# The first quarter of block 0's feed-forward done by groups of 128 tokens, the first group moved ahead of two weight scales

## Chip, cores, metric

One core of one Trainium2 chip. The metric is the device time of one execution in microseconds, the median of several runs; a profile is one more execution of the same program.

## What is computed

Causal softmax attention over 4 batches, 8 heads, 576 tokens, head width 64, mixed per head with a linear-memory read-out, and then a two-matrix feed-forward with squared ReLU over all 2304 tokens:

```
a = softmax(causal(q @ k.T / sqrt(D)));  local = a @ v
mem = (phi(q) @ M_prev) / (phi(q) @ z_prev + 1e-6)
x = (g * mem + (1 - g) * local)            # [2304, 512]
out = square(relu(x @ w_in)) @ w_out       # w_in [512, 2048], w_out [2048, 512]
```

Inputs are float32; the output must hold float32 accuracy, so the big products are made of float16 pairs (a high and a low half of each operand, three products each).

## The kernel before

**Weights.** `w_in` and `w_out` arrive as 32 pieces of 512 KB (lines 180 to 185): pieces 0 to 3 are the first quarter of the columns of `w_in`, 4 to 7 the rows of `w_out` that belong to it, 8 to 15 the second quarter, and so on. Each piece is loaded from SP's queue (`load_weight`, L273), turned to float32 on ACT and DVE (`to_float`, L198 to L203), and, four pieces at a time, PE forms a bound of the magnitudes (`gr`, L229, then L210) from which DVE makes a scale (L232 to L241). Only then `halves` (L247 on ACT, L248 on DVE) writes the float16 pair `w`. From piece 16 on the pieces use smaller rings of buffers, opened after piece 15.

**Attention.** 16 units, each a batch and a pair of heads (the first eight are cut in two by query tiles). A unit forms scores (`sp`, L586), masks them with a running maximum (L607 on DVE), exponentiates (L627 on ACT), and for the first units transposes the result on PE (`pxa`, L642), copies it (`aF`, L647 on ACT), multiplies by v (`acc`, L691) and adds into `feat` (L694). `pm` (L550) is the memory read-out. PSUM has one buffer for `sp` and two each for `up`, `acc`/`oacc` and `av`.

**Feed-forward.** `moe(n)` does a block of 256 tokens. Block 0 is the first 64 tokens of every batch, which `first_tokens` computes on its own in two groups of 128; each group's result `hl` is transposed by a DMA (L413) into its half of `xT`. Per pair of 128 hidden columns (`j`), PE does 24 products of 128x128 by 128x256 into `up` (L976 to L978), ACT does ReLU, square and a rounding to float16 (`r`, `gh`: L982, L983, L985), DVE the low half (`gl`, L988), and `down` does 12 products with 512 columns into `oacc` (L947 to L949). In block 0 every quarter (two `j`) is scaled and summed on its own (`group_sum`, L953).

**Order.** A scheduler places the instructions on each engine at build time, from the order in which the generators emit them; `ORD` (L88) merges them by ratios: attention unit 0 with half of the weight steps, then units 1 to 3 with the rest and the steps of block 0 (`first`), then the other units; blocks 1 to 8 come after. At run time each engine takes its list in order and waits where an input is late.

Of the kernel before, what the change touches and what calls it, by code (L numbers as in the profile page):

```python
# [8 lines left out]
F32 = mybir.dt.float32  # L9
F32R = mybir.dt.float32r  # L10
F16 = mybir.dt.float16
# [11 lines left out]
P = 128  # L23
# [36 lines left out]
RB = 2  # L60
# [18 lines left out]

FIRST = 4  # L80
WA = 0
WE = 8
WE2 = 40
AFTER = mybir.DependencyInfo(mybir.DependencyClass.NoSync, mybir.DependencyReason.DATA)
# [1 line left out]


def ORD(merge, attn, na, wsteps, first, order):  # L88
    merge((attn(0, 1), 12), (wsteps(17), 16))
    merge((attn(1, FIRST), 52), (wsteps(34), 16), (first(), 18))  # L90
    for _ in attn(FIRST, len(order)):
        pass

# [6 lines left out]
def fused_kernel(ctx: ExitStack, tc: tile.TileContext, t0_d, kk_d, qv_d, beta, w_in, w_out, out):  # L100
# [85 lines left out]
    def w_out_op(f, part):  # L186
        return wt[8 * (f // 4) + 4 + f % 4][:, part, :]
# [737 lines left out]
    def moe(n):  # L925
        b, blk = blocks[n]
        xT, osc = xq[n]
        x0 = xT.rearrange("p g (x b m) (h q) -> p g x b m h q", x=2, b=GB, h=2)
        pend = []

        def x_op(k, part):

            return x0[:, :, part, :, k // 2, k % 2] if lead else xT[:, :, part * NK + k]

        acc = []
        lead = b is None
        outs = []

        def down(j, gh, gl):
            if j == 0 or lead and j % 2 == 0:  # L940
                acc[:] = [ps.tile([P, DM], F32, tag="acc", name="oacc", bufs=2) for t in range(2)]
            f0, f1 = (j // 2 * 4, j // 2 * 4 + 3) if lead else (0, NF - 1)
            last = j == NF // 2 - 1 or lead and j % 2
            for u, t in [(u, t) for t in range(2) for u in range(2)] if last else [(u, t) for u in range(2) for t in range(2)]:
                f = 2 * j + u
                ts = slice(t * P, (t + 1) * P)
                nc.tensor.matmul(acc[t], gh[:, u, ts], w_out_op(f, 0), start=f == f0, stop=False)  # L947
                nc.tensor.matmul(acc[t], gh[:, u, ts], w_out_op(f, 1), start=False, stop=False)  # L948
                nc.tensor.matmul(acc[t], gl[:, u, ts], w_out_op(f, 0), start=False, stop=f == f1)  # L949
            if lead and j % 2:  # L950
                group_sum(j // 2)

        def group_sum(jj):  # L953
            kj = mo.tile([P, 2], F32, tag="kj", name="kj", bufs=2)
            kp = kap[:, jj : jj + 1]
            nc.vector.tensor_scalar(
                out=kj, in0=tok0, scalar1=kp, scalar2=kp, op0=ALU.mult, op1=ALU.mult
            )
            for t in range(2):
                if jj == 0:  # L960
                    o = mo.tile([P, DM], F32, tag="x", name="o", bufs=XB)
                    outs.append(o)
                    nc.scalar.activation(o, acc[t], AF.Copy, scale=kj[:, t : t + 1])
                else:
                    nc.vector.scalar_tensor_tensor(
                        out=outs[t], in0=acc[t], scalar=kj[:, t : t + 1], in1=outs[t], op0=ALU.mult, op1=ALU.add
                    )

        for j in range(NF // 2):
            need(1 + 8 * (j // 2 + 1))  # L970
            up = ps.tile([P, 2, BLK], F32, tag="up", name="up", bufs=2)
            for u in range(2):
                f = 2 * j + u
                uo = up[:, u].rearrange("p (g b q) -> p g b q", g=2, b=GB) if lead else up[:, u]
                for k in range(NK):
                    nc.tensor.matmul(uo, w_in_op(f, k, 0), x_op(k, 0), start=k == 0, stop=False)  # L976
                    nc.tensor.matmul(uo, w_in_op(f, k, 0), x_op(k, 1), start=False, stop=False)  # L977
                    nc.tensor.matmul(uo, w_in_op(f, k, 1), x_op(k, 0), start=False, stop=k == NK - 1)  # L978
            r = mo.tile([P, 2, BLK], F32, tag="r", name="r", bufs=RB)
            gh = mo.tile([P, 2, BLK], F16, tag="gh", name="gh", bufs=GHB)  # L980
            gl = mo.tile([P, 2, BLK], F16, tag="gl", name="gl", bufs=GLB)
            nc.scalar.activation(r, up, AF.Relu, scale=HSC if lead else gam[:, j // 2 : j // 2 + 1])  # L982
            nc.scalar.activation(r, r, AF.Square)  # L983
            if n < GHN:
                nc.scalar.copy(gh, r)  # L985
            else:
                nc.vector.tensor_copy(gh, r)
            (nc.vector if n in GLV else nc.gpsimd).tensor_tensor(out=gl, in0=r, in1=gh, op=ALU.subtract)  # L988
            pend.append((j, gh, gl))
            yield  # L990
            if len(pend) > 1:
                down(*pend.pop(0))
                yield
        for x in pend:
            down(*x)
            yield
        for t in range(2):
            if lead:
                for u in range(2):
                    r0 = (2 * t + u) * S  # L1000
                    nc.sync.dma_start(out[r0 : r0 + D, :], outs[t][u * D : (u + 1) * D])
            else:
                o = mo.tile([P, DM], F32, tag="x", name="o", bufs=XB)
                nc.scalar.activation(o, acc[t], AF.Copy, scale=osc[:, t : t + 1])
                r0 = b * S + QT[1 + 2 * blk + t][0]
                nc.sync.dma_start(out[r0 : r0 + P, :], o)
        yield
# [5 lines left out]
    def merge(*parts):  # L1013
        live = [[g, n, 0] for g, n in parts]
        while live:
            live.sort(key=lambda x: (x[2] + 0.5) / x[1])
            if next(live[0][0], "end") == "end":
                live.pop(0)
            else:
                live[0][2] += 1  # L1020
# [6 lines left out]
    def need(n):  # L1027
        while wn[0] < n:
            next(wg)
            wn[0] += 1  # L1030

    def wsteps(n):
        for k in range(n):
            if wn[0] < n:
                need(wn[0] + 1)
            yield
# [22 lines left out]
    def attn(i0, i1):  # L1059

        ahead = []
        for i in range(i0, i1):
            rows = ahead.pop() if ahead else unit(i)
            if i >= WA:
                for x in (rows,) if i == i0 else ():
                    for _ in iter(lambda: next(x), "whole"):
                        yield
                if i + 1 < i1:
                    ahead.append(unit(i + 1))
                    for _ in iter(lambda: next(ahead[0]), "whole"):  # L1070
                        yield
            yield from rows
            b, p, tiles = order[i]
            if p == NP - 1:
                need(NU + 2)
                for blk in range(2):
                    if 2 * blk + 1 in tiles and b < B - 1:
                        prefetch(b, blk)
                yield
# [65 lines left out]
```

## Time and profile before

| | |
|---|---|
| median of 3 runs | 566.0 us (564.21 to 567.09) |
| the profiled execution, own time | 562.5 us |
| its span | 560.7 us |
| PE busy | 519.1 us (93%) |
| DVE busy | 453.0 us (81%) |
| ACT busy | 410.7 us (73%) |

Busy time is a union of instructions, and a matmul's shown duration is longer than the step to the next one, since they are pipelined. A step is read from the starts of two neighbours. PEclk is the share of full speed that PE's clock was granted: 1.00 or 0.50, and a value between in a window that holds both.

### The profile page before, as it was taken

To read this page: it belongs to the slowest core of one execution; us is meant where nothing else is said; L and a number is where in the kernel's file an instruction comes from. 1 tells how busy PE (TensorE), PEld (TensorE's weight loads), DVE (VectorE), ACT (ScalarE), POOL (GpSimd) and SP (SyncE) were. 2 spreads that over 40 slices of the span, in tenths; PEclk is the share of its full clock that TensorE was granted. 3 is DMA by queue.
4 is the path that set the end of the run, shared out by engine and by line. 5 is a ranking of instruction groups with operands and counts; after the bars stand their busy time and mean duration, and the time that the engine had idled before them with its cause. 6 is when DMAs were issued, how large, how long until landed. Compare 5 with 4: busy or idle time off the path is not lost.

```text
span 560.7 us, 12604 instructions
## 1 busy us (share of the span) xinstructions
PE 519.1 (93%) x4767; PEld 367.1 (65%) x4767; DVE 453.0 (81%) x1421; ACT 410.7 (73%) x884; POOL 16.6 (3%) x20
## 2 busy tenths in 40 slices
PE   4658987999998999999989989999999999999997
PEld 3546755657676766667767757766766766447766
DVE  6898689998988889898968878887786788745645
ACT  3799899796888879799777778887576734566252
POOL 1001000011010000000000000000000000000000
PEclk9767999999999999999999999999999999999999
DMA  8952972488567657978558466482645330100002
GB/s 311 404 162 60 368 280 61 91 172 206 116 155 160 167 136 140 187 162 202 119 103 160 108 134 123 76 136 61 109 84 77 86 57 1 39 1 1 1 1 75
DMA packets 133132, 71.37 MB, mean 127 GB/s; under 512 B 115408, under 2 KB 121552, under 8 KB 133072
## 3 DMA queue, kind: packets, MB, share of 16 engines
q1 hardware_dynamic: 133072, 70.57, 52.2%
q8 instruction: 37, 0.61, 0.4%
q14 instruction: 23, 0.19, 0.1%
HBM read 37.53 MB, written 4.72 MB: 75 GB/s over the span
## 4 chain that ended last, share of the span: by engine, by line
PE 36%; DVE 29%; ACT 19%; DMA 11%; issue 3%; SPq 0%; POOL 0%; ACTq 0%; DVEq 0%
DVE e L607 5%; DVE a L667 5%; ACT e L627 5%; DMA aT<-a 4%; PE seven L844 4%; PE oacc L949 3%; PE up L976 3%; PE oacc L948 3%; PE oacc L947 3%; PE up L978 3%; PE up L977 3%; ACT a L665 3%; PE seven L815 2%; PE seven L817 2%; PE seven L816 2%
## 5 line engine op out<-in xcount | busy, mean ns | idle before, releaser
L976 PE MATMUL up<-xT,w 128*128 128x256 f16 x448 | 122.6, 274 | 0.7 <-DMA xT<-hl 0.7
L977 PE MATMUL up<-xT,w 128*128 128x256 f16 x448 | 122.6, 274 | 0.0
L978 PE MATMUL up<-xT,w 128*128 128x256 f16 x448 | 122.5, 273 | 0.0
L627 ACT ACTIVATE e<-e,mx 128x320 f32<-128x320 f32 (+3 forms) x128 | 77.4, 606 | 44.4 <-DVE feat L694 25.1
L947 PE MATMUL oacc<-w,gh 128*128 128x512 f16 x224 | 84.8, 379 | 3.4 <-ACT gh L985 3.3
L948 PE MATMUL oacc<-w,gh 128*128 128x512 f16 x224 | 84.9, 379 | 0.0
L949 PE MATMUL oacc<-w,gl 128*128 128x512 f16 x224 | 81.7, 379 | 1.4 <-DVE gl L988 1.4
L667 DVE SCALAR_TENSOR_TENSOR a<-e,a 128x128 f16<-128x128 f32 x116 | 64.6, 566 | 12.3 <-ACT a L665 11.7
L665 ACT ACTIVATE a<-e 128x128 f16<-128x128 f32 x116 | 54.9, 522 | 3.6 <-DMA aT<-a 3.3
L976 PEld LDWEIGHTS <-w 128*128 128x128 f16 x448 | 43.9, 98 | 11.1 <-DMA xT<-hl 0.8
L977 PEld LDWEIGHTS <-w 128*128 128x128 f16 x448 | 44.0, 98 | 10.6 <-issue 0.8
L691 PE MATMUL acc<-vs,aT 128*128 128x64 f16 x1138 | 42.9, 193 | 6.6 <-DMA aT<-a 5.9
L978 PEld LDWEIGHTS <-w 128*128 128x128 f16 x448 | 44.0, 98 | 6.5 <-issue 0.4
L607 DVE CUSTOM_DVE_ANT_0 e<-sp,mask 128x320 f32<-128x320 f32 (+3 forms) x128 | 47.0, 417 | 0.8 <-PE pxa L642 0.4
L691 PEld LDWEIGHTS <-aT 128*128 128x128 f16 x1138 | 38.7, 98 | 13.2 <-DMA aT<-a 8.3
L982 ACT ACTIVATE r<-up,gam 128x512 f32<-128x512 f32 x48 | 32.3, 674 | 20.2 <-PE up L978 20.1
L988 DVE TENSOR_TENSOR gl<-r,gh 128x512 f16<-128x512 f32 x56 | 38.7, 691 | 4.3 <-ACT gh L985 3.6
L949 PEld LDWEIGHTS <-gl 128*128 128x128 f16 x224 | 21.7, 98 | 24.9 <-DVE gl L988 2.6
L947 PEld LDWEIGHTS <-gh 128*128 128x128 f16 x224 | 21.9, 98 | 23.6 <-ACT gh L985 4.5
L844 PEld LDWEIGHTS <-g 128*128 128x128 f16 x336 | 32.7, 98 | 5.4 <-DVE g L770 1.2
L983 ACT ACTIVATE r<-r 128x512 f32<-128x512 f32 x56 | 34.9, 624 | 0.8
L948 PEld LDWEIGHTS <-gh 128*128 128x128 f16 x224 | 21.9, 98 | 19.8
(192 smaller groups left out, 1035.4 us busy)
## 6 DMA issues: line engine op xcount, KB each, us to landing
raw<-in_w_in_dram SPq DMA_DIRECT2D x16, 512.0 KB, 7.1
raw<-in_w_out_dram SPq DMA_DIRECT2D x16, 512.0 KB, 7.9
vv<-in_qv_dram SPq DMA_DIRECT2D x16, 320.0 KB, 3.2
kd<-in_kk_dram SPq DMA_DIRECT2D x16, 288.0 KB, 3.1
out_dram<-o SPq DMA_DIRECT2D x12, 256.0 KB, 2.2
qm<-in_qv_dram SPq DMA_DIRECT2D x8, 321.0 KB, 3.2
qm<-in_qv_dram SPq DMA_DIRECT2D x8, 193.0 KB, 2.9
vv<-in_qv_dram SPq DMA_DIRECT2D x8, 192.0 KB, 3.1
```

Of the source, the lines that this page charges most:

```text
L607: nc.vector.tensor_tensor_reduce(out=e[:, h, ka:kb], in0=sps[:, h, cs], in1=mask[:, 448 - q0 + ka : 448 - q0 + kb], scale=-0.125, scalar=3 ...
L627: ex = nc.scalar.activation(e[:n, h, :ke], e[:n, h, :ke], AF.Exp, bias=bs, scale=-1.0, accum_out=sm[:n, h : h + 1])
L665: nc.scalar.mul(av[:, :, o0 : o0 + w], x, SC)
L667: nc.vector.scalar_tensor_tensor(out=av[:, :, o0 + w : o0 + 2 * w], in0=x, scalar=SC, in1=av[:, :, o0 : o0 + w], op0=ALU.mult, op1=ALU.sub ...
L691: nc.tensor.matmul(acc[:n, h], lhs[:, :n], rhs, start=x == 0, stop=x == len(mms) - 1)
L844: mms.append(nc.tensor.matmul(x[:, blk], g[j][:, i0, a, blk, p], t_side(j, p, m, i1), start=j == js[0] and p == n == 0, stop=j == js[-1] a ...
L947: nc.tensor.matmul(acc[t], gh[:, u, ts], w_out_op(f, 0), start=f == f0, stop=False)
L948: nc.tensor.matmul(acc[t], gh[:, u, ts], w_out_op(f, 1), start=False, stop=False)
L949: nc.tensor.matmul(acc[t], gl[:, u, ts], w_out_op(f, 0), start=False, stop=f == f1)
L976: nc.tensor.matmul(uo, w_in_op(f, k, 0), x_op(k, 0), start=k == 0, stop=False)
L977: nc.tensor.matmul(uo, w_in_op(f, k, 0), x_op(k, 1), start=False, stop=False)
L978: nc.tensor.matmul(uo, w_in_op(f, k, 1), x_op(k, 0), start=False, stop=k == NK - 1)
```

## The change

Block 0's first quarter (`NQG = 1`) is done by `by_groups`: for each group of 128 tokens, 48 products with 128 moving columns into one `up` bank, the three ACT passes and the DVE pass over 128x512, then 12 products with 512 columns into an accumulator of the group's own, and its sum. Before, the same quarter was two `j` of 24 products with 256 columns. `group_sum` now takes one group at a time. `ORD` lets the first step of block 0 (the first group's `up` products and passes) come after unit 0 and 9 weight steps, that is ahead of the steps of pieces 9 to 15 in the emitted order; units 1 and 2 to 3 are merged in two separate parts.

```
+NQG = 1
 def ORD(merge, attn, na, wsteps, first, order):
-    merge((attn(0, 1), 12), (wsteps(17), 16))
-    merge((attn(1, FIRST), 52), (wsteps(34), 16), (first(), 18))
+    f = first()
+    merge((attn(0, 1), 12), (wsteps(9), 8))
+    next(f)
+    merge((attn(1, 2), 17), (wsteps(17), 8))
+    merge((attn(2, FIRST), 35), (wsteps(34), 16), (f, 17))
...
+        def by_groups(jj):
+            def sum_up(g, gh, gl):
+                y = ps.tile([P, DM], F32, tag="acc", name="accg", bufs=2)
+                for u in range(4):
+                    f = 4 * jj + u
+                    nc.tensor.matmul(y, gh[:, u], w_out_op(f, 0), start=u == 0, stop=False)
+                    nc.tensor.matmul(y, gh[:, u], w_out_op(f, 1), start=False, stop=False)
+                    nc.tensor.matmul(y, gl[:, u], w_out_op(f, 0), start=False, stop=u == 3)
+                group_sum(jj, g, y)
+            for g in range(2):
+                up = ps.tile([P, 4, P], F32, tag="up", name="upg", bufs=2)
+                for u in range(4):
+                    f = 4 * jj + u
+                    uo = up[:, u].rearrange("p (b q) -> p b q", b=GB)
+                    for k in range(NK):
+                        hi, low = (x0[:, g, x, :, k // 2, k % 2] for x in range(2))
+                        nc.tensor.matmul(uo, w_in_op(f, k, 0), hi, start=k == 0, stop=False)
+                        nc.tensor.matmul(uo, w_in_op(f, k, 0), low, start=False, stop=False)
+                        nc.tensor.matmul(uo, w_in_op(f, k, 1), hi, start=False, stop=k == NK - 1)
+                r = mo.tile([P, 4, P], F32, tag="r", name="rg", bufs=RB)
...
+                nc.scalar.activation(r, up, AF.Relu, scale=HSC)
+                nc.scalar.activation(r, r, AF.Square)
+                nc.scalar.copy(gh, r)
+                nc.vector.tensor_tensor(out=gl, in0=r, in1=gh, op=ALU.subtract)
+                yield
+                sum_up(g, gh, gl)
+                yield
...
         for j in range(NF // 2):
             need(1 + 8 * (j // 2 + 1))
+            if lead and j // 2 < NQG:
+                if j % 2 == 0:
+                    yield from by_groups(j // 2)
+                continue
```

In the built order the lists are equal up to PE's first `pm`. Line numbers of the changed kernel are higher by 4 up to `moe`; its new names end in g. Three places follow.

On PE, after unit 0's read-out `pm`, the list before goes on with the bounds of pieces 8 to 13 (`gr`, 24 products):

```order
L586 MATMUL sp<-kd,qm 128x192 x2
L550 MATMUL pm<-qm,pe 128x130 x2
L229 LDWEIGHTS fc
L229 MATMUL gr<-fc 128x128
L229 LDWEIGHTS fc
```

and of the change, at the same place:

```order
L554 MATMUL pm<-qm,pe 128x130 x2
L994 LDWEIGHTS w_488
L994 MATMUL upg<-xT,w_488 128x128
L995 LDWEIGHTS w_488
L995 MATMUL upg<-xT,w_488 128x128
L996 LDWEIGHTS w_488
L996 MATMUL upg<-xT,w_488 128x128
```

There 29 of the first group's 48 products stand now; the other 19 follow between unit 1's scores and transposes, and the first `gr` of piece 8 comes after the 48th.

On ACT, between unit 0's four exponentials and the halves of the second quarter of `w_in`, before:

```order
L627 ACTIVATE e,sm<-e,mx 128x192 x2
L416 ACTIVATE tok_80<-qn 64x1 x2
L409 ACTIVATE hl<-f,sn 128x256 x2
L647 COPY aF<-pxa 64x128 x2
L647 COPY aF<-pxa 128x256 x2
L247 ACTIVATE w_609<-fc,win_s 128x512
```

and of the change:

```order
L631 ACTIVATE e,sm<-e,mx 128x320
L1000 ACTIVATE rg<-upg 128x512
L631 ACTIVATE e,sm<-e,mx 128x320
L1001 ACTIVATE rg<-rg 128x512
L651 COPY aF<-pxa 64x128 x2
L651 COPY aF<-pxa 128x128 x2
L1002 CAST ghg<-rg 128x512
L631 ACTIVATE e,sm<-e,mx 128x192 x2
L251 ACTIVATE w_744<-fc,win_s 128x512
```

The first group's three passes, unit 1's first exponentials and unit 0's second set of copies stand ahead of the halves now.

Also on ACT, between the second quarter's halves of `w_in` and those of `w_out`, where before one followed directly on the other:

```order
L251 ACTIVATE w_753<-fc,win_s 128x512
L495 ACTIVATE pe<-qm 128x256
L968 ACTIVATE o<-accg,kj 128x512
L651 COPY aF<-pxa 64x128 x2
L651 COPY aF<-pxa 128x256
L251 ACTIVATE w_797<-fc,wout_s 128x512
```

A copy out of the first group's accumulator and copies of unit 1 came between them.

## Rows read from the trace of the kernel before

**Rows 1.** The page's parts 1 and 2: busy time, and PE in 40 slices.
```profile
PE 519.1 (93%) x4767; PEld 367.1 (65%) x4767; DVE 453.0 (81%) x1421; ACT 410.7 (73%) x884; POOL 16.6 (3%) x20
PE   4658987999998999999989989999999999999997
```
**Rows 2.** Busy time by stretch; columns: stretch, length, PE, PEld, DVE, ACT, POOL, PEclk, DMA, GB/s.
```profile
28.00:42.00 14.00, 7.32 (x70) 5.62 (x72) 13.26 (x34) 13.96 (x29) 1.12 (x1) 0.63 0.51 162
42.00:56.00 14.00, 12.59 (x82) 9.59 (x83) 12.53 (x44) 12.85 (x39) 2.64 (x2) 0.76 0.24 58
70.00:84.00 14.00, 11.90 (x93) 7.94 (x90) 11.53 (x36) 14.00 (x33) 1.30 (x1) 1.00 0.79 282
84.00:98.00 14.00, 10.82 (x82) 7.79 (x84) 13.48 (x46) 13.24 (x33) 0.00 (x0) 1.00 0.21 63
350.00:450.00 100.00, 97.64 (x987) 70.18 (x986) 77.27 (x262) 73.42 (x166) 0.00 (x0) 1.00 0.50 90
```
**Rows 3.** PE in order of time: start, length, line, operation, count, idle before.
```profile
38.24 1.40 PE L229 MATMUL gr<-fc 128*128 128x128 bf16 x16
41.82 1.98 PE L586 MATMUL sp<-kd,qm 64*128 64x320 f32 x8 [0.97 <-DVE mx L607]
50.49 0.39 PE L976 MATMUL up<-xT,w 128*128 128x256 f16 x1 [0.35 <-DMA xT<-hl]
51.10 0.42 PE L976 MATMUL up<-xT,w 128*128 128x256 f16 x1
51.32 0.42 PE L977 MATMUL up<-xT,w 128*128 128x256 f16 x1
52.41 0.27 PE L977 MATMUL up<-xT,w 128*128 128x256 f16 x1
52.52 0.27 PE L978 MATMUL up<-xT,w 128*128 128x256 f16 x1
63.07 0.63 PE L642 MATMUL pxa<-ident,e 128*64 128x128 f32 x4
65.82 0.27 PE L978 MATMUL up<-xT,w 128*128 128x256 f16 x1
79.57 1.08 PE L229 MATMUL gr<-fc 128*128 128x128 bf16 x16
107.13 0.27 PE L976 MATMUL up<-xT,w 128*128 128x256 f16 x1
```
**Rows 4.** SP's queue in order of time, and the landing of `xT`.
```profile
31.12 1.34 SPq L413 DMA_TRANSPOSE xT<-hl  x1
47.17 1.77 SPq L413 DMA_TRANSPOSE xT<-hl  x1
...
DMA to landing us min/median/max: 3.3/3.3/3.4
```
**Rows 5.** ACT in order of time, 44 to 96 us.
```profile
47.64 2.56 ACT L247 ACTIVATE w<-fc,win_s 128x512 f16<-128x512 f32 x4 [0.28 <-DVE win_s L241]
50.10 2.54 ACT L247 ACTIVATE w<-fc,wout_s 128x512 f16<-128x512 f32 x4
52.86 0.72 ACT L647 COPY aF<-pxa 64x128 f32<-64x128 f32 x4
58.63 0.60 ACT L982 ACTIVATE r<-up 128x512 f32<-128x512 f32 x1 [2.15 <-PE up L978]
59.56 0.75 ACT L198 ACTIVATE raw<-raw,under 128x512 uint32<-128x512 uint16 x1
92.77 2.57 ACT L247 ACTIVATE w<-fc,win_s 128x512 f16<-128x512 f32 x4
```
**Rows 6.** Groups of instructions by line in 0 to 150 us: count, busy us, mean ns, idle before.
```profile
L985 ACT CAST gh<-r 128x512 f16<-128x512 f32 x11 | 6.7, 610 | 0.2
L956 DVE TENSOR_SCALAR kj<-tok,kap 128x2 f32<-128x2 f32 x4 | 1.1, 286 | 0.3 <-ACT tok L416 0.3
```
**Rows 7.** The single `gr` product in the view by line: duration in ns, min/median/max.
```profile
L229 PE MATMUL gr<-fc x128: 217/218/314, 10.0 to 100.1; 128*128 128x128 bf16 x128
```

More of the change, by code (lines that the diff above doesn't have):

```diff
@@ L950, in down, with group_sum @@
             if lead and j % 2:
-                group_sum(j // 2)
-        def group_sum(jj):
-            kj = mo.tile([P, 2], F32, tag="kj", name="kj", bufs=2)
+                for t in range(2):
+                    group_sum(j // 2, t, acc[t])
+        def group_sum(jj, t, y):
+            kj = mo.tile([P, 1], F32, tag="kj", name="kj", bufs=4)
             kp = kap[:, jj : jj + 1]
             nc.vector.tensor_scalar(
-                out=kj, in0=tok0, scalar1=kp, scalar2=kp, op0=ALU.mult, op1=ALU.mult
+                out=kj, in0=tok0[:, t : t + 1], scalar1=kp, scalar2=kp, op0=ALU.mult, op1=ALU.mult
@@ L958, in group_sum @@
             )
[L959 to L967, printed above, removed]
+            if jj == 0:
+                o = mo.tile([P, DM], F32, tag="x", name="o", bufs=XB)
+                outs.append(o)
+                nc.scalar.activation(o, y, AF.Copy, scale=kj)
+            else:
+                nc.vector.scalar_tensor_tensor(
+                    out=outs[t], in0=y, scalar=kj, in1=outs[t], op0=ALU.mult, op1=ALU.add
+                )
@@ new lines, in by_groups @@
+        def by_groups(jj):
+            late = []
+            def sum_up(g, gh, gl):
[17 more added lines that the diff above has]
+                r = mo.tile([P, 4, P], F32, tag="r", name="rg", bufs=RB)
+                gh = mo.tile([P, 4, P], F16, tag="gh", name="ghg", bufs=GHB)
+                gl = mo.tile([P, 4, P], F16, tag="gl", name="glg", bufs=GLB)
+                nc.scalar.activation(r, up, AF.Relu, scale=HSC)
[5 more added lines that the diff above has]
+                yield
```

## The prediction

> **What bounds the kernel now.** I read the page's parts 1 and 2 first. PE is busy 93% of the span, DVE 81%, ACT 73% [rows 1], but the slices show that the holes of PE lie at the start. By stretches: from 350 to 450 us PE is busy 97.6 of 100, and DVE and ACT under 78 [rows 2]; what is taken from PE's idle time early is kept to the end as long as PE stays that full. From 28 to 42 us it is the other way round: PE 7.3 of 14, ACT 13.96 and DVE 13.26 [rows 2]. From 42 to 56 PE shows 12.6 of 14, but its granted clock averages 0.76 [rows 2]: a step of 256 columns there takes 0.22 us (51.10 to 51.32), and 0.11 once the clock is full (52.41 to 52.52) [rows 3]. A second hole lies from 70 to 98 us: PE 11.9 and 10.8 of 14, with ACT at 14.0 and 13.2 [rows 2]. There PE waits for weights that ACT has not yet turned into halves. So up to 100 us the kernel is bound by ACT's list (weights, with attention between), afterwards by PE.
>
> Block 0 is the only feed-forward work at hand early. Its first product starts at 50.49, 0.35 us after PE ran dry, when the second group's transposed tokens land [rows 3]; they were sent at 47.17 and land 3.3 us later [rows 4]. The first group's were sent at 31.12 [rows 4], so they are there from 34.4. The 16 us between are what the change can use.
>
> **The split itself.** Before, a quarter is 48 products of 256 columns: 48 x 0.11 = 5.3 us at the full clock [rows 3]. Now it is 96 of 128 columns, each with weights of its own. The trace has no float16 product of that size; the nearest row is `gr`, 128 columns in bfloat16, also with new weights each time: 16 take 1.08 us and one alone 0.218 [rows 3, 7], so a step is (1.08 - 0.218) / 15 = 0.057. 96 x 0.057 = 5.5 us: 0.2 more. From below it cannot be under half the columns' time, 96 x 0.055, no change; from above a step of 0.11, if a step did not shrink at all, would add 5.3. I take 0.2, from the row that is nearest.
>
> The Trainium skill speaks against the change here: "TensorE: Matmul & The Clock Gate", section "Back-to-back issue gap", gives about 81 ns per product in a sustained stream of 128-column products with weight loads. By it the 96 would take 7.8 us and the split would cost 2.5; the trace's 57 ns disagrees.
>
> The 24 `down` products keep their 512 columns; they only run as 12 and 12. ACT's passes and copies are the same in number and size. DVE gets eight small `kj` instead of four in block 0's four quarters and one more per group: 4 x 0.286 = 1.1 us at most [rows 6], less where neighbours overlap; DVE is no bound after 100 us, so I count nothing, and 1.1 if its cover is gone. SP's loads of piece 16 on now stand behind three attention loads that wait for PE's second `pm`; that comes near 54 us by the steps below, before the buffers of the second quarter come free, so nothing for that either.
>
> **What moves on PE, and its price.** All is equal up to 38.24, where 16 `gr` start [rows 3]. Now 29 group products stand there. At the low clock a step is half of 0.22, so they end by 41.3, or near 40 if the clock rises. Unit 1's scores wait for DVE until 41.82 as before and take 1.98 [rows 3]: 43.8. Then come two sets of four transposes (0.63 at the full clock, twice that at the low [rows 3]) and the other 19 products: about 47. Only then `gr`: 16 at 0.057 to 0.107, with the first `acc` between, end near 49, the other 16 and the broadcast near 51.4. On DVE one pass of the group (some 0.7) stands ahead of the scale. The second quarter's `w_in` halves, at 47.64 before [rows 5], start near 53, **5.3 later**. Its `w_out` halves, at 50.10 before [rows 5], now stand behind the copy of the first group's accumulator, which waits for 12 products of 512 columns (12 x 0.22 = 2.6) that PE reaches near 54.5: 57.1, then copies: 58.6, **8.5 later**. I expect ACT to stand idle some 1.5 us at that copy.
>
> **What hides this.** PE does not need those halves as early: it has the second group's 48 products, 12 + 12 `down` and attention to do. By my steps it is through with the 72nd product-equivalent of 256 columns at 64.6 us; before, that point is 66.1 (the last product of that run starts at 65.82 [rows 3]). By then it has also done one more set of transposes (0.63 [rows 3]) and its products with v (about 1). So PE is some **3 us ahead at 65 us**.
>
> ACT reaches piece 16's first pass later. Before: 59.56, after a wait of 2.15 for PE [rows 5]. Now four passes of a group (4 x 0.61 [rows 6]), two more sets of copies (2 x 0.72 [rows 5]) and two smaller passes (0.6) stand ahead of it, 4.5 us, and I find 4.5 us of idle between 44 and 65 against 3.2 before (2.15 of them that one wait): 59.56 + 4.5 + 1.3 = 65.4.
>
> From there to the end of the last quarter's `w_in` halves ACT needed 95.3 - 59.6 = 35.8 us [rows 5], almost without a gap. Its new list has about 4 us more attention work in that stretch (four exponentials and some `a` passes), so 65.4 + 39.8 = 105.2 if it never idles. That is 10 us later than before; but before, PE used these halves only from 107.13 [rows 3]. So PE can start the last quarter near 106, no later than before, with 3 us more of other work done. All engines have done the same work some 40 us later, and PE is full from there.
>
> **Sum:** split +0.2, work ahead -3.2: -3.0. Against the profiled execution's 562.5 this is 559.5; that execution lies 3.5 under the median of 566.0, so for the median **563.0 us**, -0.5%, just where a measurement of this kernel can tell it from no change (0.5%, 2.8 us).
>
> **Rivals.**
> - *More is kept.* The whole first group comes out of the hole (half of 5.3 for `up` and half of 24 x 0.22 for `down`, 5.2 us together), ACT's later idle shrinks too, and the clock rises earlier than 52. For it: PE's 6.7 idle us from 28 to 42 and the 0.76 clock [rows 2]. Against: ACT has no idle there to fill. -5.5: 560.5. Chance 0.20.
> - *Nothing is kept.* The 3 us run into PE's wait for weights, since ACT's total work before the last quarter is the same: 566. It needs about 3 us of idle on ACT between 65 and 105. Chance 0.17.
> - *Late weights decide: slower.* The same wait goes on growing: each scale of pieces 8 to 15 is late by 5 to 8 us, the third and fourth quarters follow on one list, and ACT stops for PE or a load as it did for 2.15 before piece 16 [rows 5]. Past some 3 us of such stops each further one is PE's too; 6.5 us (three of 2.15) make +3.5: 569.5. For it: ACT is full from 70 to 84 [rows 2], and the lists are fixed, so a late copy holds all behind it. Against: the 12 us of slack between 95.3 and 107.1. Chance 0.23.
> - *The split costs.* The group products step at 0.081 and not at 0.057: 96 x 0.024 = 2.3 on top of the forecast, 565.3. Between `gr`'s 0.057 and 0.11 such a step is possible, since `gr` reads its operand in another way. Chance 0.05. (It is the figure of the Trainium skill's page above; `gr` speaks against it.)
>
> **How the numbers follow.** The forecast has 0.35, and with later reordering, which the build changes up to the end, spreads 1.5 us to each side: half of it is faster than 0.5%. Faster: 0.20 + 0.19 = 0.39. Same: 0.16 + 0.17 + 0.05 = 0.38. Slower: 0.23. The range goes from the first rival with a us below it to the slower one, 559.5 to 569.5; the forecast's own range is 561.5 to 564.5.
>
> **What would show it.** Right: group products from 38.24, steps of 0.057 at the full clock, the second quarter's `w_in` halves near 53 and `w_out` near 58.6, piece 16's first pass near 65, the last quarter's first `up` between 104 and 107, and PE's busy share after that as before. Wrong: a wait on ACT over 3 us between 65 and 105, or `up` of the last quarter after 109 (slower); a first `up` of the last quarter before 103 (more is kept); or PE idling more after 150 us than before, where I see no cause.

## The result, and the profile after

The changed kernel takes 571.87 us (570.04 to 573.17, 4 runs) against 566.24 of the kernel before: a ratio of 1.0101, 95% interval 1.0078 to 1.0124. It is **slower by 1%**, and outside the predicted range. The profiled execution took 573.17 (span 571.4), the highest of its four, while that of before was the lowest of its own (562.5): between the two traces lie 10.7 us, between the medians 5.6. An execution that stands at the median of before comes with the experiments (null_attention_53).

The page's busy time, and PE and its clock in 40 slices [rows 1]:

```profile
PE 524.7 (92%) x4815; PEld 371.4 (65%) x4815; DVE 454.9 (80%) x1425; ACT 411.1 (72%) x884; POOL 16.0 (3%) x20
PE   4649997798999989999999999988999999999997
PEclk9969997899899989999999999999999999999999
```

Stretches of after [rows 2], with the same columns (stretch, length, PE, PEld, DVE, ACT, POOL, PEclk, DMA, GB/s):

```profile
28.00:42.00 14.00, 7.45 (x95) 6.13 (x91) 13.26 (x31) 13.96 (x27) 1.30 (x1) 0.64 0.51 167
42.00:56.00 14.00, 12.67 (x118) 10.03 (x119) 11.42 (x51) 12.29 (x42) 2.13 (x2) 1.00 0.30 76
70.00:84.00 14.00, 12.61 (x97) 8.02 (x94) 12.72 (x43) 14.00 (x34) 0.00 (x0) 1.00 0.99 376
84.00:98.00 14.00, 11.15 (x68) 7.73 (x67) 12.89 (x36) 13.85 (x33) 0.85 (x1) 0.76 0.45 122
98.00:112.00 14.00, 10.18 (x85) 6.85 (x86) 13.63 (x45) 9.40 (x18) 0.00 (x0) 0.88 0.41 97
350.00:450.00 100.00, 94.18 (x964) 67.34 (x963) 76.15 (x276) 74.67 (x172) 0.00 (x0) 1.00 0.56 98
```

The hole at 42 to 56 is better (full clock, where before had 0.76). At 84 to 98 the clock is now down, at 98 to 112 PE and ACT both have holes, and PE is 3.5 us emptier between 350 and 450, far behind the change.

PE of after in order of time [rows 3]:

```profile
38.55 0.22 PE L994 MATMUL upg<-xT,w 128*128 128x128 f16 x1
40.11 0.22 PE L995 MATMUL upg<-xT,w 128*128 128x128 f16 x1
64.21 0.27 PE L1021 MATMUL up<-xT,w 128*128 128x256 f16 x1
89.48 0.40 PE L1021 MATMUL up<-xT,w 128*128 128x256 f16 x1 [1.76 <-DVE w L252]
95.75 0.42 PE L1021 MATMUL up<-xT,w 128*128 128x256 f16 x1
95.96 0.38 PE L1019 MATMUL up<-xT,w 128*128 128x256 f16 x1
96.29 0.27 PE L1021 MATMUL up<-xT,w 128*128 128x256 f16 x1
102.69 0.39 PE L951 MATMUL oacc<-w,gh 128*128 128x512 f16 x1 [3.07 <-ACT gh L1028]
114.44 0.27 PE L1019 MATMUL up<-xT,w 128*128 128x256 f16 x1 [0.52 <-ACT r L1025]
```

and ACT [rows 5]:

```profile
52.32 2.56 ACT L251 ACTIVATE w<-fc,win_s 128x512 f16<-128x512 f32 x4 [0.30 <-DVE win_s L245]
56.48 0.69 ACT L968 ACTIVATE o<-accg,kj 128x512 f32<-128x512 f32 x1 [1.28 <-PE accg L984]
58.00 2.57 ACT L251 ACTIVATE w<-fc,wout_s 128x512 f16<-128x512 f32 x4
65.53 0.76 ACT L202 ACTIVATE raw<-raw,under 128x512 uint32<-128x512 uint16 x1
100.16 0.77 ACT L202 ACTIVATE raw<-raw,under 128x512 uint32<-128x512 uint16 x1 [2.32 <-DMA raw<-in_w_out_dram]
106.08 0.63 ACT L722 ACTIVATE hl<-feat 128x512 f16<-128x512 f32 x1 [2.24 <-DVE feat L698]
107.33 2.54 ACT L251 ACTIVATE w<-fc,win_s 128x512 f16<-128x512 f32 x4
```

Up to 65.53 ACT is where the prediction put it. The last quarter's halves come at 107.33 (92.77 before) and its first product at 114.44 (107.13 before).

### The profile page after: what moved, and what is told of

The parts are those of the page before. It is cut to its first block, busy times and chain, and to the rows that moved or that the text cites. A ratio compares the mean times of both kernels' runs of the same rounds, so it can differ in the third digit from the quotient of the medians.

```text
span 571.4 us, 12712 instructions
## 1 busy us (share of the span) xinstructions
PE 524.7 (92%) x4815; PEld 371.4 (65%) x4815; DVE 454.9 (80%) x1425; ACT 411.1 (72%) x884; POOL 16.0 (3%) x20
## 4 chain that ended last, share of the span: by engine, by line
PE 55%; ACT 17%; DVE 13%; DMA 12%; issue 2%; SPq 0%; POOL 0%; ACTq 0%; DVEq 0%
DMA aT<-a 7%; PE oacc L952 6%; PE oacc L953 6%; PE up L1019 6%; PE oacc L951 6%; PE up L1021 6%; PE up L1020 6%; PE acc L695 5%; PE sp L590 5%; PE seven L848 3%; ACT e L631 3%; DVE g L774 2%; DVE a L671 2%; ACT raw L205 2%; ACT raw L202 2%
## 5 line engine op out<-in xcount | busy, mean ns | idle before, releaser
L1021 PE MATMUL up<-xT,w 128*128 128x256 f16 x432 | 119.4, 276 | 2.1 <-DVE w L252 2.1
L1019 PE MATMUL up<-xT,w 128*128 128x256 f16 x432 | 119.6, 277 | 0.5 <-ACT r L1025 0.5
L1020 PE MATMUL up<-xT,w 128*128 128x256 f16 x432 | 119.3, 276 | 0.0
L951 PE MATMUL oacc<-w,gh 128*128 128x512 f16 x216 | 82.7, 383 | 4.1 <-ACT gh L1028 4.1
L952 PE MATMUL oacc<-w,gh 128*128 128x512 f16 x216 | 83.0, 384 | 0.0
L953 PE MATMUL oacc<-w,gl 128*128 128x512 f16 x216 | 79.6, 383 | 0.9 <-DVE vy L523 0.9
L671 DVE SCALAR_TENSOR_TENSOR a<-e,a 128x128 f16<-128x128 f32 x116 | 65.6, 579 | 12.5 <-ACT a L669 12.1
L1020 PEld LDWEIGHTS <-w 128*128 128x128 f16 x432 | 43.0, 99 | 11.0 <-issue 1.3
L1019 PEld LDWEIGHTS <-w 128*128 128x128 f16 x432 | 42.9, 99 | 10.9 <-issue 0.8
L1021 PEld LDWEIGHTS <-w 128*128 128x128 f16 x432 | 42.9, 99 | 9.9 <-DVE w L252 2.9
L1025 ACT ACTIVATE r<-up,gam 128x512 f32<-128x512 f32 x48 | 32.4, 674 | 19.2 <-PE up L1021 19.1
L1031 DVE TENSOR_TENSOR gl<-r,gh 128x512 f16<-128x512 f32 x54 | 37.1, 688 | 7.4 <-ACT gh L1028 6.8
L951 PEld LDWEIGHTS <-gh 128*128 128x128 f16 x216 | 21.3, 99 | 23.3 <-ACT gh L1028 4.8
L698 DVE SCALAR_TENSOR_TENSOR feat<-acc,sm,feat 128x64 f32<-128x64 f32 x128 | 29.6, 279 | 6.2 <-PE acc L695 6.1
L1026 ACT ACTIVATE r<-r 128x512 f32<-128x512 f32 x54 | 33.7, 623 | 0.6
```

The lines of the kernel that those rows point to most:

```text
L671: nc.vector.scalar_tensor_tensor(out=av[:, :, o0 + w : o0 + 2 * w], in0=x, scalar=SC, in1=av[:, :, o0 : o0 + w], op0=ALU.mult, op1=ALU.sub ...
```

## The experiments

One measure is used throughout, **PE's loss in a stretch**: the length less busy time times granted clock, added up over steps of 1 us. Idle time and a low clock both count. It is taken from 28 us on, since the clock's records begin only at 7.6 to 21.6 us, depending on the trace (last section). There is one trace per kernel, and two executions of one order can differ by some 4 us in a stretch (below).

| kernel | us, median (lowest to highest) | 28-56 | 56-84 | 84-112 | 112-450 |
|---|---|---|---|---|---|
| before (profiled: 562.5) | 566.2 (564.2 to 567.1) | 13.9 | 2.1 | 4.0 | 10.7 |
| changed | 571.9 (570.0 to 573.2) | 10.5 | 1.4 | 11.6 | 18.1 |
| *no groups:* null_attention_53 | 566.2 (563.7 to 568.7) | 15.5 | 0.8 | 6.1 | 11.8 |
| null_first_17 | 572.8 (571.2 to 574.3) | 13.9 | 2.2 | 6.0 | 18.0 |
| before_54 | 574.0 (573.4 to 574.4) | 15.2 | 1.2 | 6.8 | 17.9 |
| before_21 | 581.0 (579.0 to 583.0) | 14.1 | 1.8 | 10.2 | 20.0 |
| ratios_only | 576.6 (573.0 to 578.4) | 16.1 | 4.8 | 7.6 | 17.1 |
| late_order_of_after | 574.6 (572.5 to 575.7) | 15.4 | 1.0 | 7.3 | 19.3 |
| *split, not early:* split_only | 576.6 (575.2 to 577.8) | 11.0 | 2.9 | 7.1 | 21.8 |
| split_rest_as_before | 570.2 (568.3 to 570.5) | 11.5 | 4.3 | 6.3 | 16.6 |
| *early groups:* passes_behind_halves | 576.6 (574.0 to 582.1) | 11.7 | 3.0 | 10.1 | 17.6 |
| own_queue | 592.3 (589.5 to 592.7) | 11.6 | 9.7 | 16.0 | 21.8 |
| null_after_36 | 576.5 (576.2 to 578.0) | 10.5 | 1.3 | 15.1 | 19.1 |
| seven_raw_buffers | 572.3 (570.7 to 575.0) | 10.3 | 0.9 | 11.7 | 18.0 |
| late_order_of_before | 572.0 (568.4 to 574.3) | 10.5 | 1.3 | 9.5 | 19.8 |
| rest_as_before | 580.4 (578.5 to 585.1) | 10.6 | 9.8 | 12.2 | 20.5 |
| after_33 | 571.5 (568.4 to 576.0) | 10.2 | 1.4 | 12.2 | 13.6 |
| after_21 | 572.3 (571.3 to 573.9) | 10.3 | 1.5 | 12.5 | 17.8 |
| after_16 | 576.9 (574.8 to 578.2) | 11.6 | 1.4 | 14.5 | 16.6 |
| after_15 | 571.1 (568.5 to 571.6) | 11.7 | 2.9 | 12.9 | 11.8 |

The kernel before stood at 565.2 to 566.3 beside each batch.

### Parts of the change

Theory A took the loss for the groups' own: the weights behind them come late. Four kernels took the change apart.

**split_only.** The groups, at the place in the merges where the first quarter stood before:

```diff
-    f = first()
-    merge((attn(0, 1), 12), (wsteps(9), 8))
-    next(f)
-    merge((attn(1, 2), 17), (wsteps(17), 8))
-    merge((attn(2, FIRST), 35), (wsteps(34), 16), (f, 17))
+    merge((attn(0, 1), 12), (wsteps(17), 16))
+    merge((attn(1, FIRST), 52), (wsteps(34), 16), (first(), 18))
```

> The quarter is done by groups of 128 tokens, but in the order of emission of the kernel before (block 0 merged in after 17 weight steps), so on ACT the halves of the second quarter come ahead of the groups' passes again. Theory A (the early group makes the weights late): halves of the last quarter of w_in start below 97 us, 566 us, within 2.5 of the kernel before. Rival B (the merge of attention ahead of the weights is what costs): the same, 566. Rival C (the split itself costs, by products of 128 columns or by its separate sums): 571, and a step of the group products well over 0.057 us.

Measured 1.0193 (1.0169 to 1.0216), slower than the whole change. The second quarter's `w_in` halves come at 48.44 and hardly late, the group products step by 0.056, yet the loss behind 112 us doubles.

**ratios_only.** The kernel before with the new merges and no group:

```diff
-    merge((attn(0, 1), 12), (wsteps(17), 16))
-    merge((attn(1, FIRST), 52), (wsteps(34), 16), (first(), 18))
+    f = first()
+    merge((attn(0, 1), 12), (wsteps(9), 8))
+    merge((attn(1, 2), 17), (wsteps(17), 8))
+    merge((attn(2, FIRST), 35), (wsteps(34), 16), (f, 18))
```

> The kernel before with 256-column products throughout, but with the changed merges of attention and weight steps (9 steps with unit 0, 8 more with unit 1, the rest with units 2 and 3) and no early step of block 0. Theory A: 566, within 2.5 of before, since no group pass stands ahead of the halves. Rival B: 570 to 572, the whole loss. Rival C: 566.

Measured 1.0190 (1.0161 to 1.0218). Each part alone costs about 10.8, more than both together: prices that don't add up are no prices of parts. From 155 us on the two traces even show the same order of instructions.

**passes_behind_halves.** The change, with the first group's Relu held behind the last half of piece 15 (the products and the passes are two steps there, so the merge has 18 for 17):

```diff
...
+                if g == 0:
+                    tc.add_manual_dep(rl.ins, half[15].ins.name, AFTER, reason="passes behind the halves")
```

> The changed kernel, with the first group's 48 products as early as there, but its three ACT passes held behind the last half of piece 15. Theory A: the w_out halves of the second quarter come some 3 us earlier than in the changed kernel (its wait for the first accumulator is gone), and the time falls to 567 or 568. Rival B: 571, as the merges are unchanged. Rival C: 571.

Measured 1.0202 (1.0159 to 1.0245). The halves came at 51.85 and 57.80, no more than half a us sooner than in the changed kernel: it isn't these passes that hold them. The wait that the edit meant to move hardly moved, so it says nothing on its price.

**own_queue.** The raw loads of pieces 16 to 31 on GpSimd's queue, out of the way of the attention's loads:

```diff
-        nc.sync.dma_start(raw[n], w[r0 : r0 + P, cs])
+        (nc.gpsimd if n >= NR0 else nc.sync).dma_start(raw[n], w[r0 : r0 + P, cs])
```

> The changed kernel, with the loads of pieces 16 to 31 on GpSimd's queue, so that they wait for their buffers alone and not behind attention's loads on SP's. Theory A in full (late halves, and then loads of the last pieces stuck on SP behind attention's): ACT's wait of 2.3 us for a w_out piece near 98 us goes, the last quarter's first product comes 2 to 4 us before the 114.4 of the changed kernel, 568 or 569. If the queue is only beside the path: 571 to 572, same as the changed kernel.

Measured 1.0456 (1.0429 to 1.0484). From this view of ACT's waits from 60 to 130 us (what waited, for what: us in total, times, longest) the edit brought a price of its own, 28.0 us of waits for raw pieces (2.3 in the changed kernel), and leaves the question open:

```profile
ACT raw L202 <- DMA raw<-in_w_out_dram: 8.9, 4, 2.8
ACT raw L205 <- DMA raw<-in_w_in_dram: 8.2, 3, 2.9
ACT raw L202 <- DMA raw<-in_w_in_dram: 5.6, 3, 2.5
ACT raw L205 <- DMA raw<-in_w_out_dram: 5.3, 2, 3.1
```

GpSimd issued the first loads at 61.12, 65.65, 69.79 and 74.32, one by one, and they landed 3.8 us later in the median; in the changed kernel SyncE sent four in 2.79 us.

### Changes that change nothing

All four missed, so a second theory, D: the builder settles every queue anew behind any edit, and it is leaving the order of the kernel before that costs. One number of a merge, no work added or taken, tests it. The edits, in this order: in the kernel before 52 to 53, and 18 to 17; in the changed kernel 35 to 36; and six buffers to seven, which brings the `w_out` loads forward:

```diff
-    merge((attn(1, FIRST), 52), (wsteps(34), 16), (first(), 18))
+    merge((attn(1, FIRST), 53), (wsteps(34), 16), (first(), 18))
...
+    merge((attn(1, FIRST), 52), (wsteps(34), 16), (first(), 17))
...
-    merge((attn(2, FIRST), 35), (wsteps(34), 16), (f, 17))
+    merge((attn(2, FIRST), 36), (wsteps(34), 16), (f, 17))
...
-NRAW2 = 6
+NRAW2 = 7
```

> The kernel before with one number of its merge changed: the attention's share of the opening is 53 steps where it was 52. No instruction is added or taken away, and the group ahead of the scales isn't there; a few instructions change places with their neighbours. Theory A (the whole loss of the change comes from what the early groups make late, the weights of the last quarter): the time stays within 2.5 us of the kernel before, 563.5 to 568.5, and the first pass of the last quarter starts at 107 us, give or take 2. Theory D (the order that the kernel before was built with is an uncommonly good one, and most ways of leaving it cost several us, whatever they are for): 568 to 578.

> The kernel before with one other number of its merge changed: the first block's share is 17 steps where it was 18, as in the change, and nothing else. No instruction is added or taken away. Theory A: 563.5 to 568.5, the first pass of the last quarter at 107 us, give or take 2. Theory D: 568 to 578.

> The changed kernel with one number changed: the attention's share of the third merge is 36 steps where it was 35. Groups, work and their early place stay as in the change. Theory A: within 2.5 us of the changed kernel, 569.5 to 574.5, and the first pass of the last quarter near 114 us. Theory D: the time moves by more than 2.5 us either way, anywhere from 564 to 579, and the order of the runs by time needn't follow when the last quarter starts.

> The changed kernel with seven buffers for the raw pieces 16 to 31 where it has six, so that SyncE's queue issues each load one piece sooner, and the last w_out loads ahead of two of the attention's vv loads. Theory A: ACT no longer waits 2.3 us for a w_out piece near 98, the halves of the last quarter's w_in come at 101 to 104 (107.3 in the changed kernel), its first pass at 107 to 110 (114.4), and the time falls to 566 to 569. Theory D: the early places come sooner or not, and the time is anywhere from 566 to 579 without following them.

null_attention_53: 0.9996 (0.9972 to 1.0020). Its order differs from that of before in a few rows of ACT and SyncE between 66 and 77 us alone and is the same to the end, so it shares that order, and its profiled execution, 566.36, is a typical one of it. null_first_17: 1.0124 (1.0093 to 1.0156). It is equal to before up to 77 us on PE and 90 on ACT and differs from there to far behind 450. That alone costs 6.5 us, as much as the change. Stretches of null_attention_53, null_first_17 and the changed kernel, and PE's waits of the first two from 112 to 450 us:

```profile
84.00:112.00 28.00, 24.72 (x195) 17.60 (x194) 27.20 (x89) 24.35 (x58) 0.85 (x1) 0.88 0.36 88
112.00:450.00 338.00, 327.85 (x3251) 234.74 (x3250) 287.02 (x1026) 268.85 (x615) 8.26 (x7) 0.99 0.64 132
```

```profile
84.00:112.00 28.00, 23.75 (x187) 17.01 (x188) 25.41 (x86) 20.91 (x50) 1.02 (x1) 0.94 0.28 69
112.00:450.00 338.00, 321.65 (x3195) 226.43 (x3194) 279.96 (x1017) 264.34 (x609) 7.76 (x7) 0.99 0.67 132
```

```profile
84.00:112.00 28.00, 21.33 (x153) 14.58 (x153) 26.52 (x80) 23.25 (x51) 0.85 (x1) 0.82 0.43 109
112.00:450.00 338.00, 324.72 (x3192) 232.40 (x3191) 278.46 (x996) 261.78 (x599) 8.33 (x7) 0.98 0.66 129
```

```profile
PE acc L691 <- DMA aT<-a: 4.6, 8, 1.6
PE oacc L947 <- ACT gh L985: 1.8, 2, 1.1
PE oacc L949 <- DVE gl L988: 1.4, 1, 1.4
```

```profile
PE acc L691 <- DMA aT<-a: 6.5, 7, 1.3
PE oacc L947 <- ACT gh L985: 4.1, 4, 2.6
PE sp L586 <- DVE mx L607: 3.9, 5, 2.2
```

PE is busy 327.85 of 338 us in the one and 321.65 in the other: 6.2 between them, near the 6.5 of the medians. No single wait makes it; a handful of waits of 1 to 3 us, for a transposed `a`, a `gh`, a bound `mx`, do.

null_after_36: 1.0189 (1.0160 to 1.0217), 4.6 above the changed kernel with the same groups. seven_raw_buffers: 1.0121 (1.0084 to 1.0158), as the changed kernel, though its early places came as theory A wanted: ACT no longer waits for a piece, and the last quarter's halves begin at 99.38, 8 us sooner. PE then waits for something else, and loses 11.7 between 84 and 112 as before:

```profile
99.38 2.58 ACT L251 ACTIVATE w<-fc,win_s 128x512 f16<-128x512 f32 x4
```

```profile
98.35 1.57 PE L695 MATMUL acc<-vs,aT 128*128 128x64 f16 x26 [2.18 <-DMA aT<-a]
102.67 2.19 PE L590 MATMUL sp<-kd,qm 64*128 64x448 f32 x8 [2.75 <-DVE mx L611]
114.66 0.27 PE L1019 MATMUL up<-xT,w 128*128 128x256 f16 x1 [1.46 <-ACT r L1025]
```

So the late loads of `w_out` are not the cause of that hole. Theory A falls as the whole story. The edit also did what nobody asked of it: from 154 us on, this kernel's PE, ACT, DVE and SyncE go through the order of the kernel before. That matters below.

### Holding an order

Whether it is the later order as such was tested by holding it. All that comes from the fifth attention unit on is the same 5544 instructions in both programs; 5533 of them are chained, engine by engine, in the order of the other kernel, with no wait between engines added:

```diff
+    late = nc.cur_bb.bb.instructions[mark[-1] :]
+    for steps in json.loads(zlib.decompress(base64.b85decode("".join(LATE_ORDER.split())))).values():
+        n, x = 0, None
+        for d in steps:
+            n += d
+            if x is not None:
+                tc.add_manual_dep(late[n], x.name, AFTER, reason="the order of the other kernel")
+            x = late[n]
```

> The changed kernel, whose 5533 instructions of everything from the fifth attention unit on are held, engine by engine (PE, ACT, DVE, SP), in the order that they have in the kernel before; the instructions ahead of them, the groups among these, are as in the change. Theory L (the groups' gain is given back by 112 us and no more than that, and the rest of the loss comes from the order of the later blocks, which the builder settles anew behind any change): 565 to 568, with idle plus slow-clock loss of PE from 140 to 450 us near 9.5 us (15.8 in the changed kernel). Theory A (what the early groups make late costs the 5.6 us by itself): 570 to 573, the later blocks running as far behind as they start.

> The kernel before, without groups, whose 5533 instructions from the fifth attention unit on are held in the order that they have in the changed kernel. Theory L: 569 to 574, slower than the kernel before by 3 us or more though nothing of the change's early part is in it, with idle plus slow-clock loss of PE from 140 to 450 us at 13 us or more (9 to 9.5 in the kernel before). Theory A: 564 to 568.

Measured 1.0086 (1.0055 to 1.0118) and 1.0144 (1.0124 to 1.0164). The second came out as theory L said: no group, and 8.3 us slower. The first refutes it: the later order of before, put back behind the groups, gives nothing back (572.0), and loses 19.8 us from 112 on where it lost 10.7 and 11.8 behind its own opening. So it is not a good order for itself. It may be that any order is slow behind an opening that it wasn't settled with; then the second run, which is such a pair too, says nothing of the order of after by itself.

Then all but the first quarter's own work was held in the order of before, in the changed kernel and in split_only, by the same chain over the whole program (SyncE from the start, ACT and DVE from about 58 us, PE from the first pass of the third quarter; further ahead the groups stand in the way):

> The changed kernel, in which all that is not the first quarter's own work is held in the order of the kernel before: SyncE's loads from the start, ACT and DVE from about 58 us on, PE from the first pass of the third quarter (81 us there) to the end. Only the groups stand elsewhere. Theory O (what costs is not the groups but that every later queue is settled anew): the gain of some 3 us at 56 to 65 us survives, 561 to 565. Theory M (the groups take ACT and DVE from the weights at 40 to 60 us, and the time that the weights lose there comes back at the last quarter whatever the order): 568 to 575, with the last quarter's first pass at 112 us or later.

> The kernel with the split alone (its groups where the first quarter stood before), in which the rest is held in the order of the kernel before in the same way. Its earlier form, in an order settled anew, took 576.6. Theory O: 564 to 568, no slower than the kernel before by over 2 us. Theory M: 570 or more, since the split's passes and its two more accumulators are still there.

Measured 1.0275 (1.0234 to 1.0316) and 1.0068 (1.0044 to 1.0092). The split gains 6.4 us by the held order (576.6 to 570.2), so most of its price went with the order; 4.8 stay, with no early group. With the early groups it fails, and for a reason of its own. In ACT's held list a pass of block 0 stands behind halves, and ACT waits 4.41 for a bound and 3.68 for a load ahead of them; PE waits 6.6 for that pass, as its row shows:

```profile
94.52 0.37 PE L1070 MATMUL up<-xT,w 128*128 128x256 f16 x1 [6.57 <-ACT r L1076]
```

So it can't say whether the gain would survive an order without that wait.

### More orders, with and without groups

If the order costs, orders without the group must lie as high as those with it. Two more of each sort, then two more with the group; the edits are 52 to 54 and 18 to 21 in the kernel before, 35 to 33 and 17 to 21, 16, 15 in the changed one, in the merge lines shown above.

> The kernel before with the attention's share at 54 steps where it was 52; ACT's order differs from its 120th row on, the last quarter's time, and to the end. No group, no work changed. Theory G (the groups cost): 564 to 569. Theory D (the order costs): 570 to 578.

> The kernel before with the first block's share at 21 steps where it was 18; ACT's order differs from its 105th row on, the third quarter's time, and to the end. No group, no work changed. Theory G: 564 to 569. Theory D: 570 to 578.

> The changed kernel with the attention's share of its third merge at 33 steps where it was 35: four rows of ACT and four of DVE change places, in the last quarter's time, SyncE's order stays. Theory G: within 2.5 us of the changed kernel, 569.4 to 574.4. Theory D: so few rows moved, also near the changed kernel, 568 to 576; if it moves by more than 2.5 us, even four rows do it.

> The changed kernel with the first block's share at 21 steps where it was 17: some 40 rows of ACT and 120 of DVE change places from the third quarter on. Theory G: 569.4 to 574.4 or more, and not below 569, for the groups stay. Theory D: anywhere from 563 to 578.

> The changed kernel with the first block's share at 16 steps where it was 17; ACT's order differs from its 163rd row on, the last quarter's time. Theory D (orders of this kind lie over 571 to 577, the first kernel's 566 being the best of its kind by chance or by search): 569 to 577, with a small chance of under 566. Theory G (the groups cost): 570 to 575, never under 566.

> The changed kernel with the first block's share at 15 steps where it was 17; ACT's order differs from its 93rd row on, the time of the second quarter's halves. Theory D: 569 to 580, with a small chance of under 566. Theory G: 570 or more.

Ratios: 1.0147 (1.0091 to 1.0203), 1.0271 (1.0212 to 1.0330), 1.0110 (1.0041 to 1.0179), 1.0120 (1.0070 to 1.0171), 1.0178 (1.0144 to 1.0212), 1.0073 (1.0053 to 1.0092). Theory G, that it is the groups that cost, expected the first two at 564 to 569; they took 574.0 and 581.0, 8.8 and 15.8 above the kernel before beside them. So an order alone can cost as much as the change and more.

These are fewer orders than runs. Row by row (operation, tiles, shapes) the traces show the same order in null_first_17 and before_54 but for three rows of ACT, in null_after_36 and after_16 throughout, and in the changed kernel and after_33 but for two neighbouring rows of PE; after_21 goes as the changed kernel from 144 us on. Such pairs show the scatter: after_33's executions run from 568.4 to 576.0, and behind 112 us its trace lost 13.6 where that of the changed kernel lost 18.1. So without the groups two orders other than that of before were measured, not three.

The same later order, from 180 us at the latest, was also run with and without groups:

| later order | no groups | split, not early | early groups |
|---|---|---|---|
| of before | 566.2, 566.2 | 570.2 | 572.3 (seven_raw_buffers), 572.0, 580.4 (both held) |
| of the changed kernel | 574.6 (held) | | 571.9, 571.5, 572.3 |
| of null_first_17 | 572.8, 574.0 | | 576.6 (passes_behind_halves) |
| of ratios_only | 576.6 | 576.6 | |

Behind the order of before the early groups add 6 us, behind that of null_first_17 some 3; behind that of the changed kernel they take some 3 off (580.4 has the stop shown above). So neither the groups nor the later order has a price of its own, and the kernel before is the one fast pair. In the first row of the table, PE's way through the same rows can be compared from 154 us on, null_attention_53 ahead of seven_raw_buffers each time:

```profile
155.00 0.38 PE L947 MATMUL oacc<-w,gh 128*128 128x512 f16 x1
157.44 0.38 PE L951 MATMUL oacc<-w,gh 128*128 128x512 f16 x1
```

```profile
423.10 1.63 PE L691 MATMUL acc<-vs,aT 128*128 128x64 f16 x50 [0.64 <-DMA aT<-a]
427.39 2.27 PE L695 MATMUL acc<-vs,aT 128*128 128x64 f16 x50 [1.69 <-DMA aT<-a]
```

```profile
454.82 0.38 PE L947 MATMUL oacc<-w,gh 128*128 128x512 f16 x1
460.62 0.38 PE L951 MATMUL oacc<-w,gh 128*128 128x512 f16 x1
```

Behind the groups PE begins 2.4 us late and ends 5.8 late (late_order_of_before: 3.1 and 7.0). Of what it loses on the way, 2.6 (2.7) come at the middle row and right behind it: the wait for a transposed `a` is 1.69 (1.82) and the granted clock of 420 to 450 is 0.94 in both, where null_attention_53 waits 0.64 and has 1.00. Why that `a` comes later was not found.

No order with groups came under 566, so no run beats the kernel before; the lowest is split_rest_as_before at 570.2.

## Why the prediction was wrong

**Right: everything up to 65 us.** The group products start at 38.55 and step by 0.056 (29 from 38.55 to 40.11; 0.057 predicted), so the rival in which they step at 0.081 falls. The Trainium skill ("TensorE: Matmul & The Clock Gate", "Back-to-back issue gap") gives that figure, about 81 ns, for such a stream; the trace disagrees with it. The halves come at 52.32 and 58.00 (53 and 58.6), ACT idles 1.28 at the copy (1.5), piece 16's first pass stands at 65.53 (65.4), and the last product of the first two quarters ends at 64.48 (64.6). PE's loss from 28 to 56 is 10.5 against 13.9 and 15.5 in two executions with the order of before, and 10.2 to 11.7 in all ten other kernels with early groups: the gain is real, 3.4 to 5.0 where 3 were forecast. But split_only and split_rest_as_before have 11.0 and 11.5 there too, so most of it goes with the groups of 128 wherever they stand; what the early place adds is that less is lost again from 56 to 84 (1.4 against 2.9 and 4.3). And the mark itself scatters by as much as the gain: the last product of the first two quarters starts at 64.21, at 65.82 in the trace that was read, and at 68.88 in null_attention_53, with the same PE order up to there.

**Wrong, the first step: "All engines have done the same work some 40 us later, and PE is full from there."** The gain is gone by 112 us. From 84 to 112 the changed kernel loses 11.6, the order of before 4.0 and 6.1, and none of the kernels with early groups is under 9.5. "105.2 if it never idles" was the weak link: ACT is idle 4.6 us between 98 and 112 (9.40 of 14), 2.32 of it for a load and 2.24 for `feat`; the halves end these 4.6 us later, at 109.87, and the last quarter starts at 114.44 and not "near 106". I treated ACT's list as the only bound and DVE as a neighbour; the lower halves and `feat` on DVE's list are what PE and ACT wait for by name (1.76 for `w`, 2.24 for `feat`). From 28 to 112 the losses add up to 23.5, against 20.0 and 22.4 in the order of before: this is the rival "nothing is kept", or a little worse. What sets it was not found. A full DVE alone doesn't explain it: from 84 to 112 DVE is busy 26.52 of 28 in the changed kernel, 26.74 in seven_raw_buffers, and 26.74 and 27.20 with the order of before, which loses a third to a half as much. Where the groups stand ahead of the later order of before, PE is 2.4 and 3.1 us behind at 155 us and not 3 ahead, by the rows above, and further behind at 455: PE was not "full from there".

**Wrong, the second step: "with later reordering, which the build changes up to the end, spreads 1.5 us to each side".** I saw the reordering and gave it a width without a row for it, and no sign. Two orders with nothing else changed measured 6.5 and 8.8 (one order, twice) and 15.8 above the kernel before beside them, none below it. Against the typical execution of before (null_attention_53, span 564.6) the changed kernel's 6.8 us come apart by stage: about -0.7 up to 28, -5.0 from 28 to 56, +0.6, +5.5 from 84 to 112, and **+6.3 from 112 to 450**. So the stretch that the prediction worked out comes to about nothing, and the slowdown stands behind it, where the prediction had no term but this width. null_first_17 loses as much there (18.0 against 11.8) without any group.

That the new order is what slowed the changed kernel is not shown, though. With the order of before from 154 us on, settled freely or held, it takes 572.3 and 572.0, as in its own. Both steps failed; how the 5.6 us divide between them stays open, and since neither has a price of its own (table of orders), they may not divide at all.

**The rivals.** "Late weights decide" named the right direction and its mark (the last quarter's product after 109), and two of ACT's stops of the kind it names were there (2.32 for a load, 2.24 for `feat`), not the three of its sum; but with the first removed in seven_raw_buffers the time stayed, and that its 569.5 comes nearest of all the rivals is luck, since most of the loss lies behind 112 us. My last sentence of what would be wrong, "PE idling more after 150 us than before, where I see no cause", is what happened.

**Open.** Why a kernel loses 11 us from 112 on or 17 to 22. Only before, null_attention_53 and after_15 (11.8) are at the low end, and after_15 lost 27.5 between 28 and 112 us, so that it ends at 571.1 all the same; after_33, with the order of the changed kernel, has 13.6. The order of before is low only behind its own opening, which speaks for a fit of the whole, but that is argued: no cause was isolated.

## What to carry to other kernels

Where a builder settles the order of thousands of later instructions, an edit's price contains a term for the new order, and it can be larger than the edit. Measure it first, with edits that change only the order, check in the traces which of them really gave a new order, and give a prediction that width, towards slower when the kernel at hand is the best of the orders tried. Do not add up parts of a change in such a program: compare one later order with and without the part, and more than one order, since the part's price can change its sign from one to the next. And take the scatter of the marks from several executions of the kernel before, not from the one that was profiled.

## What was not expected of the hardware

The granted clock is part of the price of a wait. In the changed kernel PE stood 1.76 us, and the products of 256 columns from 89.48 on step by some 0.21 us, the level of 1.2 GHz, until 96.29, from where they step by 0.11 again; the stretch shows 0.76. In null_first_17 PE stood 2.30 at 88.42; there the products of 512 columns step by 0.43 from 89.76 to 92.32, and at 93.15 those of 256 step by 0.11 again, so the clock was low for about half as long, behind a longer wait. The length of the wait doesn't give the length of the low clock.

The granted clock of the opening can't be read from every trace. The first 28 us are the same instructions in the same order in the kernel before and in null_first_17; from 12 to 20 us the one shows 0.50 and the other 1.00:

```profile
12.00:20.00 8.00, 5.68 (x85) 4.89 (x82) 7.13 (x20) 4.93 (x9) 0.00 (x0) 0.50 1.02 409
12.00:20.00 8.00, 5.84 (x86) 4.91 (x82) 7.09 (x20) 4.96 (x9) 0.00 (x0) 1.00 1.03 411
```

```profile
12.84 0.61 PE L229 MATMUL gr<-fc 128*128 128x128 bf16 x4
12.83 0.61 PE L229 MATMUL gr<-fc 128*128 128x128 bf16 x4
```

(the kernel before first). But four `gr` take 0.61 in both, and 0.40 at 24.38 and 24.35, where both traces show 1.00: the clock was low in both, and null_first_17 has no record of it ahead of 21.42. A stretch without a record counts as 1.00. The starts of rows show how far openings differ: unit 0's first `sp` stands at 35.21, 35.18, 36.29 and 36.02 in before, null_first_17, null_attention_53 and before_54, and the last product of the first two quarters at 65.82, 65.85, 68.88 and 67.94.
